# The head of a fused attention and feed-forward kernel: passes of one, two and two chunks, x loaded first, and a shorter warm-up

## The chip, the cores and the metric

The kernel runs on one core of a Trainium2 chip. The metric is the device time of one execution in microseconds (us). The engines are TensorE (PE, with its weight loads shown apart as PEld), VectorE (DVE), ScalarE (ACT), GpSimd (POOL) and SyncE (SP). SyncE computes nothing here: it issues the transfers between the chip's memory (DRAM) and SBUF, one after another, from one queue.

## The reference

x has 2048 tokens of 640 values, in bf16. Two branches work on the same x, and a gate mixes them by token:

```python
g = _sigmoid((x * gate_w).sum(-1, keepdims=True))
a = _A_ref(x, A_wqkv, A_w_phi, A_wo)      # linear attention, 32 heads of 20
b = _B_ref(x, B_w_gate, B_w_up, B_w_down) # (silu(x @ w_gate) * (x @ w_up)) @ w_down
return g * a + (1 - g) * b
```

Branch A projects x to q, k and v, multiplies q and k by a small matrix for each head, takes softmax of the result and of its negative as features, forms the feature-by-value matrix of each head over all tokens, and divides numerator by denominator for each token before the output projection `wo`. Branch B is a feed-forward layer with 1728 hidden values, which the kernel cuts into 14 tiles of up to 128.

## The kernel before, in words

The tokens are worked on in four blocks of 512. 640 values are 5 chunks of 128 rows, so a product with x for one hidden tile is 5 matmuls of 128x512 accumulated in one PSUM bank (of 8). x reaches SBUF transposed as `xT[128, chunk, token]`, by transposing transfers that SyncE issues (`load_x`, L509). The gate and up weights stand in `wg` and `wu` as `[128, chunk, column]`; `load_gu` (L504) loads them in pieces of columns, and the first 512 columns, four hidden tiles, are loaded by `load_head` (L532).

A small planner written in Python (`_Plan`, L237) fixes the order of the instructions on every engine when the program is built. Each task has an engine, a planned cost, dependencies, a priority, and PSUM banks or buffers that it takes and gives back. The planner simulates time: on each engine it takes the ready task of the best priority. A load has a planned landing time (`land`), and for landings over 13 us an extra slack (`L_SLACK`); `E_SLACK` and `O_SLACK` (L483) are extra time for the transposes inside the chip, of the features (`eT`) and of the attention output (`oT`). The Q and K tiles may not start before `K_AT + K_EACH * t` and `Q_AT + Q_EACH * t` (L707, L853). Only the order that comes out of this enters the program: on the chip, engines wait on semaphores for data that is truly there, not for planned times.

The stages, as the profile shows them: a warm-up of TensorE on a row of ones (L603 to L615), ten matmuls of 512 columns whose results nobody reads, from 0.8 us; the **head** (`ffn_head`, L677), the gate and up products of the first token block for the first four hidden tiles, 40 matmuls in 8 banks, until 13.8 us; further feed-forward tiles with the premultiplied projections; from about 30 us V and K tiles, with feed-forward tiles filling TensorE; from about 121 us Q tiles with numerator, output projection and down projections. Results are stored tile by tile to the end.

The order within the head is written out by hand. `group(key, c0, c1, parts)` makes a TensorE task for each tuple of hidden tiles in `parts`; a task runs the chunks c0 to c1 of its tiles, and waits for x of its last chunk and for its weights. The tasks are chained by `after`, so they run in the order written: gate chunks 0-1 for four tiles, up chunks 0-1 for four tiles, gate chunks 2-3 then 4 for tiles 0 and 1, gate chunks 2-4 for tiles 2 and 3, up chunks 2-4 tile by tile (L697 to L702). Behind them `ffn_tail` (L629) empties the banks: tanh of the gate and a copy of the up product on ACT, a combination on DVE, the product on POOL.

SyncE's queue starts with (L538 to L545): gate weights of chunks 0-1, x chunks 0-1, up weights of chunks 0-1, gate weights of chunks 2-4 for two tiles, x chunks 2-3, x chunk 4, gate weights of chunks 2-4 for the other two tiles, up weights of chunks 2-4, then the next piece of gate and up weights, and x of the second token block. The order follows the priorities, and `load` chains the loads of one engine.

All matmuls of the kernel other than the warm-up carry line L442 in the profile, all transfers L470, and most ACT operations L452.

Of the kernel before, what the change touches and what calls it, by code (L numbers as in the profile page):

```python
# [6 lines left out]
P = 128  # L7
# [29 lines left out]
class _Tracker:  # L37
# [123 lines left out]
    def run(self, eng, fn, reads=(), writes=(), semname=None, inc=None):  # L161
        rkeys = [self._key_of(a) for a in reads]
        wkeys = [self._key_of(a) for a in writes]
        need = {}

        def req(ev):
            if ev is None:
                return
            s, v = ev
            if v > need.get(s, 0):  # L170
                need[s] = v

        for k in rkeys:
            for kk in self._conflicts(k):
                req(self.lastw[kk])
        for k in wkeys:
            for kk in self._conflicts(k):
                req(self.lastw[kk])
                for s, v in self.readers[kk].items():
                    req((s, v))  # L180
        self._emit_waits(eng, need)
        ins = fn()
        if semname is None:
            semname = {"pe": "pe", "act": "act", "dve": "dve", "pool": "pool"}[eng]
            if inc is None:
                inc = 1
        elif semname == "dma":
            semname = self.new_dma_sem()
            inc = 16
        ins.then_inc(self.sem[semname], inc)  # L190
        self.cnt[semname] += inc
        v = self.cnt[semname]
        ev = (semname, v)
        snapd = dict(self.known[eng])
        if snapd.get(semname, 0) < v:
            snapd[semname] = v
        self.evknow.setdefault(semname, {})[v] = snapd
        for k in wkeys:
            self.lastw[k] = ev
            self.readers[k] = {}  # L200
        for k in rkeys:
            r = self.readers[k]
            if r.get(semname, 0) < v:
                r[semname] = v
        return ev
# [31 lines left out]
class _Plan:  # L237
# [11 lines left out]
    def add(self, eng, cost, fn, deps=(), prio=5.0, lat=None, acq=(), rel=(), name=""):  # L249
        t = _Task(eng, cost, fn, deps, prio, self.LAT[eng] if lat is None else lat,  # L250
                  tuple(acq), tuple(rel), len(self.tasks), name)
        self.tasks.append(t)
        return t
# [82 lines left out]
def _mm(*cols):  # L336
    return sum(c / 2400.0 + 0.003 for c in cols)


def _build(  # L340
# [13 lines left out]
    pe, act, dve, pool, sp = nc.tensor, nc.scalar, nc.vector, nc.gpsimd, nc.sync  # L354
    run = tr.run
# [54 lines left out]
    ps = nc.alloc_psum_tensor("ps", [P, 8 * 512], F32)  # L410
# [6 lines left out]
    add = plan.add  # L417
# [4 lines left out]
    def one(b, c0, c1, r0=0, r1=P):  # L422
        return ps[r0:r1, b * 512 + c0:b * 512 + c1]
# [4 lines left out]
    def mms(groups):  # L428

        reads = [g[1] for g in groups] + [g[2] for g in groups]  # L430
        writes = []
        seen = set()
        for g in groups:
            k = (g[0].offset, str(g[0].ap))
            if k not in seen:
                seen.add(k)
                writes.append(g[0])

        def fn():
            last = None  # L440
            for o, l, r, st, sp_ in groups:
                last = pe.matmul(o, lhsT=l, rhs=r, start=st, stop=sp_, skip_group_check=True)  # L442
            return last
        run("pe", fn, reads=reads, writes=writes)
# [21 lines left out]
    def dma(eng, dst, src, transpose=False, keep=False):  # L466
        eobj = tr.engobj[eng]
        reads = [src] if src.tensor.name in tr.addr else []
        writes = [dst] if dst.tensor.name in tr.addr else []
        fn = (lambda: eobj.dma_start(dst, src, transpose=True)) if transpose else (lambda: eobj.dma_start(dst, src))  # L470
        ev = run(eng, fn, reads=reads, writes=writes, semname="dma")
        if keep:
            out_evs.append(ev)
# [6 lines left out]
    v1ones = places(v1all)[:, :, :, DH]  # L480
    v1pad = v1all.rearrange("p (g x) -> p g x", x=WIN)[:, :, WIN - 1]

    L_SLACK, E_SLACK, O_SLACK = 1.0, 1.4, 1.0  # L483
    chain = {}

    def load(eng, dst, src, land, prio, transpose=False, name="load", cost=0.06):

        t = add(eng, cost, lambda: dma(eng, dst, src, transpose=transpose), prio=prio, lat=2.0, name=name)
        t.land = land
        t.slack = L_SLACK if land > 13 else 0.0  # L490
        t.after = chain.get(eng)
        chain[eng] = t
        return t
# [7 lines left out]
    wgl = [None] * (NPC + 1)  # L501
    wul = [None] * (NPC + 1)

    def load_gu(j, eng, land, prio):  # L504
        c0, c1 = PIECES[j]
        wgl[j] = load(eng, wg[:, :, c0:c1], gsrc[:, :, c0:c1], land[0], prio)
        wul[j] = load(eng, wu[:, :, c0:c1], usrc[:, :, c0:c1], land[1], prio + 0.1)

    def load_x(bt, prio, *cuts):  # L509

        tok = slice(512 * bt, 512 * bt + 512)
        out_ = []
        for i, (c0, c1, land) in enumerate(cuts):
            out_ += [load("sp", xT[:, c0:c1, tok], x2[tok, c0 * P:c1 * P], land, prio + 0.1 * i, True, "x%d" % bt)] * (c1 - c0)
        return out_
# [12 lines left out]
    xs = [None] * NBT  # L528
    HD = 4
    hw = {}  # L530

    def load_head(key, c0, c1, k0, k1, land, prio):  # L532
        w, src = (wg, gsrc) if key == "g" else (wu, usrc)
        t = load("sp", w[:, c0:c1, k0 * P:k1 * P], src[:, c0:c1, k0 * P:k1 * P], land, prio)
        for k in range(k0, k1):
            hw[key, c0, k] = t
        return t
    load_head("g", 0, 2, 0, HD, 3.9, -43)  # L538
    xa = load_x(0, -42, (0, 2, 5.25))
    load_head("u", 0, 2, 0, HD, 6.9, -41)  # L540
    load_head("g", 2, 5, 0, 2, 7.4, -40.5)
    xs[0] = xa + load_x(0, -40, (2, 4, 8.8), (4, 5, 9.3))
    wgl[0] = load_head("g", 2, 5, 2, HD, 10.0, -39.5)
    wul[0] = load_head("u", 2, 5, 0, HD, 11.3, -39)
    load_gu(1, "sp", (12.5, 13.7), -37)  # L545
    xs[1] = load_x(1, -36.5, (0, 5, 16.4))
    ph_l = load("sp", wph[:, :, :], rows(A_w_phi.rearrange("h e f -> (h e) f")), 16.5, -36.2)
    load_gu(2, "sp", (17.6, 18.8), -36)
# [51 lines left out]

    ones_row = nc.const_aps.tensor(1.0, (P, 512), BF16)

    def warm(banks, before):  # L603
        ctx = {}

        def fn():
            for b in banks:
                last = pe.matmul(one(b, 0, 512), lhsT=ones_row[:, 0:P], rhs=ones_row[:, 0:512], start=True, stop=True, skip_group_check=True)
            return last
        b0, b1 = min(banks), max(banks) + 1  # L610
        t = add("pe", 0.427 * len(banks), lambda: run("pe", fn, reads=[], writes=[ps[:, b0 * 512:b1 * 512]]), prio=-10,
                acq=[("bank", ctx, i) for i in range(b0, b1)], rel=[("bank", ctx, i) for i in range(b0, b1)], name="warm")
        t.after = before
        return t
    warm_t = warm((4, 5, 6, 7, 4, 5), warm((0, 1, 2, 3), None))  # L615


    gate_t = {}
# [58 lines left out]
    def ffn_head():  # L677
        tsl = slice(0, 512)
        cs = [{} for _ in range(HD)]
        before = warm_t  # L680
        last = {}

        def group(key, c0, c1, parts):
            nonlocal before
            w = wg if key == "g" else wu

            def fn(ks, cc):
                mms([(one(cs[k][key], 0, 512), w[:, c, P * k:P * k + P], xT[:, c, tsl], c == 0, c == 4) for c in cc for k in ks])
            for ks in parts:
                t = add("pe", _mm(*[512] * (len(ks) * (c1 - c0))), lambda ks=ks: fn(ks, range(c0, c1)),  # L690
                        deps=[xs[0][c1 - 1], hw[key, min(c0, 2), ks[-1]]], prio=-5,
                        acq=[("bank", cs[k], key) for k in ks] if c0 == 0 else (), name="head")
                t.after = before
                before = t
                for k in ks:
                    last[key, k] = t
        group("g", 0, 2, [(0, 1, 2, 3)])  # L697
        group("u", 0, 2, [(0, 1, 2, 3)])
        group("g", 2, 4, [(0, 1)])
        group("g", 4, 5, [(0, 1)])  # L700
        group("g", 2, 5, [(2, 3)])
        group("u", 2, 5, [(0,), (1,), (2,), (3,)])  # L702
        for k in range(HD):
            ffn_tail(0, k, cs[k], (last["g", k], last["u", k]), 0)

    B_FIRST = 8
    K_AT, K_EACH, Q_AT, Q_EACH = 30.0, 6.08, 120.8, 8.05  # L707
    PRE_Q = 10.06
    PRE_EACH = 2.2
    PRE_AT = 23.6  # L710
# [305 lines left out]
    pre_q = premult(0, wqT_l, PRE_Q, 0.02)  # L1016
    wq_done[0] = pre_q[-1]
    ffn_head()
    for bt in range(NBT):
        for t in range(4 * bt, 4 * bt + 4):  # L1020
# [6 lines left out]
    for bt in range(1, NBT):  # L1027
        ks = list(range(K_PAIRS if bt == 1 else 0, NK))
# [72 lines left out]
```

## Time and profile before

| | |
|---|---|
| median of 3 runs | 287.67 us (287.45 to 287.74) |
| span of the profiled execution, first to last instruction | 285.6 us |
| time of that execution outside the span | not listed; the median is 2.07 us over the span |
| TensorE busy | 282.2 us, 99% of the span |
| first matmul of the warm-up | 0.84 us |
| first matmul of the head | 5.17 us |
| first matmul after the head | 13.80 us |
| granted clock of TensorE, mean | 1.000 |

Times inside the profile are counted from the start of the span. A matmul's listed length holds its way through the array, and the next one starts before it ends; the pace is read from the starts. A transfer's instruction on SyncE (SPq) shows only its issue; its data move later, and the time "to landing" runs from the start of the issue to the last increment of its semaphore. "Idle before" names what ended an engine's idle time.

### The profile page before, as it was taken

How to read it: one execution, taken by the hardware profiler on the slowest of the kernel's cores; microseconds unless marked ns; L12 is line 12 of the kernel's file. 1: busy time of each engine (PE TensorE's matmuls, PEld its weight loads, DVE VectorE, ACT ScalarE, POOL GpSimd, SP SyncE). 2: the span in 40 equal slices, each digit the busy share in tenths (PEclk: the TensorE clock that was granted, in tenths of full speed). 3: DMA queues.
4: the chain of work that ended last, by engine and by line, in shares of the span. 5: the costliest groups of instructions: out<-in, count | busy, mean ns of one | idle time of the engine just before them, and what ended most of it. 6: DMA issues, size and time to landing. Idle time of an engine off the chain costs nothing.

```text
span 285.6 us, 5119 instructions
## 1 busy us (share of the span) xinstructions
PE 282.2 (99%) x2050; PEld 151.0 (53%) x2050; DVE 223.9 (78%) x318; ACT 146.2 (51%) x222; POOL 171.2 (60%) x164
## 2 busy tenths in 40 slices
PE   8999999999999999999999999999999999999996
PEld 3445555455555555655445555555455565545654
DVE  1324299999999999999999977989999978970312
ACT  2555656775756584344563454456655545564110
POOL 5199407686388748663684577676986666665100
DMA  7999999200000000000217517363435335323211
GB/s 178 258 234 268 225 187 330 88 1 1 2 0 2 0 0 2 2 0 0 45 20 82 127 50 143 75 95 76 93 79 96 67 66 117 60 39 75 69 48 46
DMA packets 65848, 23.91 MB, mean 84 GB/s; under 512 B 53984, under 2 KB 65824, under 8 KB 65824
## 3 DMA queue, kind: packets, MB, share of 16 engines
q1 hardware_dynamic: 65168, 23.58, 38.5%
q8 instruction: 16, 0.26, 0.4%
q10 hardware_dynamic: 656, 0.00, 0.1%
q14 instruction: 8, 0.07, 0.1%
HBM read 8.30 MB, written 2.62 MB: 38 GB/s over the span
## 4 chain that ended last, share of the span: by engine, by line
PE 97%; DMA 1%; SPq 0%; DVE 0%; issue 0%
PE ps L442 97%; DMA xT<-in_A_x_dram 1%; SPq L470 0%; DVE xsb L738 0%
## 5 line engine op out<-in xcount | busy, mean ns | idle before, releaser
L905 POOL TENSOR_TENSOR phi<-phi,rc 128x1320 bf16<-128x1320 bf16 x32 | 77.6, 2426 | 37.8 <-DVE rc L899 37.7
L654 POOL TENSOR_TENSOR hT<-hT,us 128x512 bf16<-128x512 bf16 (+1 forms) x56 | 64.1, 1154 | 41.8 <-DVE hT L648 21.2
L442 PE MATMUL ps<-xT,wg 128*128 128x512 bf16 x280 | 69.1, 379 | 0.2 <-DMA xT<-in_A_x_dram 0.2
L442 PE MATMUL ps<-xT,wu 128*128 128x512 bf16 x260 | 64.3, 379 | 0.0
L442 PE MATMUL ps<-wd,hT 128*128 128x512 bf16 (+1 forms) x448 | 63.0, 299 | 0.0
L648 DVE SCALAR_TENSOR_TENSOR hT<-hT,ps 128x512 bf16<-128x512 bf16 (+1 forms) x56 | 37.5, 674 | 20.4 <-ACT hT L452 20.4
L895 DVE TENSOR_REDUCE sm<-phi 128x66 f32<-128x1320 bf16 x32 | 48.5, 1517 | 6.2 <-ACT phi L452 6.0
L452 ACT ACTIVATE phi<-phi 128x1320 bf16<-128x1320 bf16 x32 | 41.6, 1301 | 17.9 <-DVE phi L884 17.6
L452 ACT ACTIVATE hT<-ps 128x512 bf16<-128x512 f32 (+1 forms) x56 | 33.1, 594 | 34.1 <-PE ps L442 33.6
L442 PEld LDWEIGHTS ps<-wd,hT 128*128 128x128 bf16 x448 | 35.0, 98 | 26.9
L442 PE MATMUL ps<-wqk,xT 128*128 128x512 bf16 (+1 forms) x320 | 48.5, 299 | 0.0
L452 ACT ACTIVATE us<-ps 128x512 bf16<-128x512 f32 (+1 forms) x56 | 33.2, 597 | 17.2 <-PE ps L442 15.7
L442 PEld LDWEIGHTS ps<-xT,wu 128*128 128x128 bf16 x260 | 25.3, 98 | 30.9 <-issue 0.3
L442 PEld LDWEIGHTS ps<-xT,wg 128*128 128x128 bf16 x280 | 25.7, 98 | 25.9 <-issue 0.8
L442 PEld LDWEIGHTS ps<-wqk,xT 128*128 128x128 bf16 x320 | 26.2, 98 | 21.2 <-ACT hT L452 0.2
L872 DVE TENSOR_REDUCE mx<-ps 128x33 f32<-128x660 f32 x32 | 26.8, 837 | 9.3 <-PE ps L442 9.2
L452 ACT ACTIVATE xsb<-ps,gs 128x640 bf16<-128x640 f32 x16 | 12.7, 795 | 32.3 <-PE ps L442 32.3
L884 DVE TENSOR_TENSOR phi<-mn,ps 128x660 bf16<-128x660 f32 x32 | 26.3, 821 | 0.4
L880 DVE TENSOR_TENSOR phi<-ps,mx 128x660 bf16<-128x660 f32 x32 | 26.3, 821 | 0.0
L876 DVE TENSOR_REDUCE mn<-ps 128x33 f32<-128x660 f32 x32 | 26.2, 819 | 0.0
L752 POOL TENSOR_TENSOR xsb<-xsb,xb 128x640 bf16<-128x640 bf16 x12 | 16.7, 1395 | 14.3 <-ACT xb L452 14.3
L442 PE MATMUL ps<-wo,oT 128*128 128x512 bf16 (+1 forms) x160 | 24.3, 299 | 0.0
(44 smaller groups left out, 187.9 us busy)
## 6 DMA issues: line engine op xcount, KB each, us to landing
out_dram<-xsb SPq DMA_DIRECT2D x15, 160.0 KB, 2.0
wd<-in_B_w_down_dram SPq DMA_DIRECT2D x1, 2080.0 KB, 9.4
wg<-in_B_w_gate_dram SPq DMA_DIRECT2D x2, 400.0 KB, 4.1
wu<-in_B_w_up_dram SPq DMA_DIRECT2D x2, 400.0 KB, 4.9
wvg<-in_A_wqkv_dram SPq DMA_DIRECT2D x1, 800.0 KB, 6.9
wo<-in_A_wo_dram SPq DMA_DIRECT2D x1, 800.0 KB, 10.7
wg<-in_B_w_gate_dram SPq DMA_DIRECT2D x2, 320.0 KB, 4.2
wu<-in_B_w_up_dram SPq DMA_DIRECT2D x2, 320.0 KB, 4.8
```

The costliest lines, as they stand in the source:

```text
L442: last = pe.matmul(o, lhsT=l, rhs=r, start=st, stop=sp_, skip_group_check=True)
L452: run("act", lambda: act.activation(o, i, func, scale=scale), reads=reads, writes=[o])
L648: dveop(lambda: dve.scalar_tensor_tensor(out=hap, in0=hap, scalar=1.0, in1=g_, op0=ALU.add, op1=ALU.mult), [hap, g_], [hap])
L654: poolop(lambda: pool.tensor_tensor(hap, hap, u_, ALU.mult), [hap, u_], [hap])
L752: poolop(lambda: pool.tensor_tensor(x_, x_, b_, ALU.add), [x_, b_], [x_])
L872: dveop(lambda: dve.tensor_reduce(a, b, AX.X, ALU.max), [b], [a])
L876: dveop(lambda: dve.tensor_reduce(a, b, AX.X, ALU.min), [b], [a])
L880: dveop(lambda: dve.tensor_tensor(o_, a, b, ALU.subtract), [a, mx[:, ctx["st"], :]], [o_])
L884: dveop(lambda: dve.tensor_tensor(o_, a, b, ALU.subtract), [b, mn[:, ctx["st"], :]], [o_])
L895: dveop(lambda: dve.tensor_reduce(a, b, AX.X, ALU.add), [b], [a])
L905: poolop(lambda: pool.tensor_tensor(a, a, b, ALU.mult), [a, r], [a])
```

## The change

The five chunks of the head are worked on in three passes: chunk 0, chunks 1-2, chunks 3-4, each with the gate product before the up product, for all four hidden tiles. The loads are cut at the same places, 9 in place of 8: x, gate weights, up weights of each pass in turn, x first. All are still issued by SyncE. The warm-up has 8 matmuls of 384 columns in place of 10 of 512. The planned landing times, the planned cost of the first gate pass, `E_SLACK`, `O_SLACK`, and the holds of the K and Q tiles get new values, and the planner makes a new order from them.

```diff
-    L_SLACK, E_SLACK, O_SLACK = 1.0, 1.4, 1.0
+    L_SLACK, E_SLACK, O_SLACK = 1.0, 1.6, 1.4
...
-    def load_head(key, c0, c1, k0, k1, land, prio):
+    HEAD_C = (0, 1, 3, 5)
+
+    def load_head(eng, key, i, land, prio):
         w, src = (wg, gsrc) if key == "g" else (wu, usrc)
-        t = load("sp", w[:, c0:c1, k0 * P:k1 * P], src[:, c0:c1, k0 * P:k1 * P], land, prio)
-        for k in range(k0, k1):
-            hw[key, c0, k] = t
-        return t
-    load_head("g", 0, 2, 0, HD, 3.9, -43)
-    xa = load_x(0, -42, (0, 2, 5.25))
-    load_head("u", 0, 2, 0, HD, 6.9, -41)
-    load_head("g", 2, 5, 0, 2, 7.4, -40.5)
-    xs[0] = xa + load_x(0, -40, (2, 4, 8.8), (4, 5, 9.3))
-    wgl[0] = load_head("g", 2, 5, 2, HD, 10.0, -39.5)
-    wul[0] = load_head("u", 2, 5, 0, HD, 11.3, -39)
-    load_gu(1, "sp", (12.5, 13.7), -37)
+        c0, c1 = HEAD_C[i], HEAD_C[i + 1]
+        hw[key, i] = load(eng, w[:, c0:c1, 0:HD * P], src[:, c0:c1, 0:HD * P], land, prio, cost=0.5 if eng == "act" else 0.06)
+        return hw[key, i]
+    xs[0] = load_x(0, -43, (0, 1, 3.6))
+    load_head("sp", "g", 0, 4.0, -42.5)
+    load_head("sp", "u", 0, 4.6, -42.4)
+    xs[0] = xs[0] + load_x(0, -42, (1, 3, 5.9))
+    load_head("sp", "g", 1, 6.4, -41)
+    load_head("sp", "u", 1, 7.0, -40.5)
+    xs[0] = xs[0] + load_x(0, -40, (3, 5, 8.2))
+    wgl[0] = load_head("sp", "g", 2, 8.9, -39.5)
+    wul[0] = load_head("sp", "u", 2, 9.5, -39)
+    load_gu(1, "sp", (11.5, 12.7), -37)
...
+    WARM_N = 384
...
-                last = pe.matmul(one(b, 0, 512), lhsT=ones_row[:, 0:P], rhs=ones_row[:, 0:512], start=True, stop=True, skip_group_check=True)
+                last = pe.matmul(one(b, 0, WARM_N), lhsT=ones_row[:, 0:P], rhs=ones_row[:, 0:WARM_N], start=True, stop=True, skip_group_check=True)
...
-        t = add("pe", 0.427 * len(banks), lambda: run("pe", fn, reads=[], writes=[ps[:, b0 * 512:b1 * 512]]), prio=-10,
+        t = add("pe", 0.32 * len(banks), lambda: run("pe", fn, reads=[], writes=[ps[:, b0 * 512:b1 * 512]]), prio=-10,
...
-    warm_t = warm((4, 5, 6, 7, 4, 5), warm((0, 1, 2, 3), None))
+    warm_t = warm((4, 5, 6, 7), warm((0, 1, 2, 3), None))
...
+            i = HEAD_C.index(c0)
             for ks in parts:
-                t = add("pe", _mm(*[512] * (len(ks) * (c1 - c0))), lambda ks=ks: fn(ks, range(c0, c1)),
-                        deps=[xs[0][c1 - 1], hw[key, min(c0, 2), ks[-1]]], prio=-5,
+                t = add("pe", _mm(*[512] * (len(ks) * (c1 - c0))) * (1.0 if c0 or key == "u" else 1.6), lambda ks=ks: fn(ks, range(c0, c1)),
+                        deps=[xs[0][c1 - 1], hw[key, i]], prio=-5,
...
-        group("g", 0, 2, [(0, 1, 2, 3)])
-        group("u", 0, 2, [(0, 1, 2, 3)])
-        group("g", 2, 4, [(0, 1)])
-        group("g", 4, 5, [(0, 1)])
-        group("g", 2, 5, [(2, 3)])
-        group("u", 2, 5, [(0,), (1,), (2,), (3,)])
+        for i in range(2):
+            for key in "gu":
+                group(key, HEAD_C[i], HEAD_C[i + 1], [(0, 1, 2, 3)])
+        group("g", 3, 5, [(0, 1), (2, 3)])
+        group("u", 3, 5, [(0,), (1,), (2,), (3,)])
...
-    K_AT, K_EACH, Q_AT, Q_EACH = 30.0, 6.08, 120.8, 8.05
+    K_AT, K_EACH, Q_AT, Q_EACH = 30.00, 6.147, 121.50, 8.058
```

## The prediction, made before the changed kernel ran

> **What bounds the kernel now.** I read the page's first line of busy times, then the chain that ended last, then the PE waits, and only then the timeline of the head.
>
> ```profile
> span 285.6 us, 5119 instructions
> PE 282.2 (99%) x2050; PEld 151.0 (53%) x2050; DVE 223.9 (78%) x318; ACT 146.2 (51%) x222; POOL 171.2 (60%) x164
> ```
>
> ```profile
> 1.32 3.72 DMA xT<-in_A_x_dram
> 5.04 0.14 issue
> 5.17 278.13 PE ps L442 x2040
> 283.31 0.02 issue
> 283.33 0.35 DVE xsb L738
> ```
>
> The chain says it all: one transfer of x lands at 5.04, and from 5.17 to 283.31 TensorE runs 2040 matmuls with nothing between them. The list of PE waits has only two entries, 0.8 us before the warm-up and 0.2 us for that x. So the time is (moment at which useful matmuls start) + 278.1 us of matmuls + a tail of 2.3 us + any idle time or half-speed time that PE gets after its start. The diff changes no useful matmul, so only the start, and idle or slow time after it, can move the end. The whole time of the profiled execution is not listed beside its span; the median of the three runs, 287.67, is 2.07 us over the span. I take these 2.07 us as unchanged and add differences to 287.67. A measurement of this kernel can tell about 0.2% (0.57 us) from no change.
>
> The stage that the diff rewrites, in the timeline (start, length, engine, what):
>
> ```profile
> 0.80 0.45 SPq L470 DMA_DIRECT2D wg<-in_B_w_gate_dram  x1
> 0.84 4.09 PE L608 MATMUL ps<-const-bfloat16-1.0 128*128 128x512 bf16 x10 [0.84 <-PEq L1085]
> 1.32 1.32 SPq L470 DMA_TRANSPOSE xT<-in_A_x_dram  x1
> 2.69 0.57 SPq L470 DMA_DIRECT2D wu<-in_B_w_up_dram  x1
> 3.31 0.46 SPq L470 DMA_DIRECT2D wg<-in_B_w_gate_dram  x1
> 3.82 2.53 SPq L470 DMA_TRANSPOSE xT<-in_A_x_dram  x2
> 5.17 1.89 PE L442 MATMUL ps<-xT,wg 128*128 128x512 bf16 x8 [0.24 <-DMA xT<-in_A_x_dram]
> 6.90 1.89 PE L442 MATMUL ps<-xT,wu 128*128 128x512 bf16 x8
> 8.65 4.80 SPq L470 DMA_TRANSPOSE xT<-in_A_x_dram  x1
> 13.80 1.24 PE L442 MATMUL ps<-xT,wg 128*128 128x512 bf16 x5
> ```
>
> Two rates come from here. Eight head matmuls start every 1.73 us (5.17 to 6.90), 0.216 us each, and the head's 40 take 8.63 us, until 13.80. And SyncE, which issues every load, needs 1.2 to 1.3 us for a transpose whether it holds one chunk of x or two (1.32 for two; 2.53 for one of two and one of one), and 0.45 to 0.58 us for a plain load.
>
> **The part that starts earlier.** The change's first load is x chunk 0. Laid out with these issue times (1.26 for a transpose, 0.57 for a plain load after one, 0.48 for the next, 0.05 between): x0 issued at 0.80, g0 at 2.11, u0 at 2.73, x1-2 at 3.25, g1-2 at 4.53, u1-2 at 5.15, x3-4 at 5.68, g3-4 at 6.97, u3-4 at 7.60. How long from issue to landing?
>
> ```profile
> out_dram<-xsb SPq DMA_DIRECT2D x15, 160.0 KB, 2.0
> wg<-in_B_w_gate_dram SPq DMA_DIRECT2D x1, 256.0 KB, 2.9
> wu<-in_B_w_up_dram SPq DMA_DIRECT2D x1, 256.0 KB, 3.4
> out_dram<-xsb SPq DMA_DIRECT2D x1, 128.0 KB, 1.7
> ```
>
> The 256 KB rows are today's first gate load (nothing ahead of it) and first up load (behind a transpose). No load of 128 KB exists; the nearest rows are the output stores, 1.7 us for 128 KB and 2.0 for 160 KB. For g0 and u0 (128 KB) I take 1.95, with ends 1.7 and 2.9. So g0 lands at 4.06 (3.8 to 5.0), x0 long before it (a transpose of five blocks, oT, lands after 2.6 us, so about 3.4), and the first useful matmul starts at 4.2, given the 0.13 us between landing and matmul seen above (5.04 to 5.17). u0 lands at 2.73 + 1.95 = 4.7, before the gate pass ends. PE therefore starts 0.97 us earlier. If nothing else happened, that would be the gain.
>
> **The part that is late next.** The first two passes hold only 4 + 4 matmuls now, 1.73 us at full speed, where before they held 8 + 8 (3.46 us). PE is through them at 5.9 to 6.4. The next pass needs x1-2 and g1-2. x1-2 is issued at 3.25 and would land 2.9 us later at 6.15 (an unhindered transpose of eleven blocks, eT, takes 3.5 to 3.6 in its rows, of five blocks 2.6; eight blocks lie between). g1-2 is 256 KB issued at 4.53. Its bounds are 2.0 us (the 160 KB store) and 3.4 us (the up load behind a transpose, which is its exact position). I take 2.4: the store's 2.0 plus 96 KB more at the 234 to 311 GB/s that the DMA windows of the head show, 0.3 to 0.4 us. I choose it nearer to the store because the queues ahead of it are emptier than they were for today's up load: only 640 KB are issued before it, and SyncE's issue time leaves holes. So g1-2 lands at 6.93 (6.5 to 7.9) and its matmuls start at 7.06 (6.7 to 8.1). 32 matmuls are left, 6.91 us: the head ends at **13.97** (13.6 to 15.0) against 13.80, which is **+0.17 us** (-0.2 to +1.2). Later passes do not bind: u1-2, issued at 5.15, is needed at 8.8; g3-4 (6.97) at 10.5, u3-4 (7.60) at 12.2, each 3.5 us or more after issue. So the 0.97 us gained at the start come back as a hole of about 0.7 to 1.1 us before the second gate pass.
>
> **What the shorter warm-up costs.** Today the ten warm-up matmuls start 0.427 us apart (two of them span 1.06 us from 3.36) until the ninth; the tenth follows 0.34 us after it, and useful matmuls run at 0.216 from the first. So PE went to full speed at about 4.46, 3.6 us after its first matmul, though the column of the granted clock reads 1.00 all along:
>
> ```profile
> 0.80:4.20 3.40, 3.36 (x8) 1.00 0.70 151
> 4.20:4.60 0.40, 0.40 (x3) 1.00 0.99 162
> ```
>
> With eight matmuls of 384 columns (0.427 x 384/512 = 0.32 each) the warm-up ends at 0.84 + 2.56 = 3.4, and PE rests 0.8 us until 4.2. If full speed still comes at 4.46, the useful matmuls lose (4.46 - 4.2)/2 = 0.13 us; if it comes later, half of each further microsecond. But the hole before 7.06 hides it: the two small passes end at 5.93 plus half the slow time, so slowness until 6.46 costs nothing. I put this term at 0, under the cover of the late g1-2 load; without the cover it is 0.13 to 0.5 us. The diff's own planning cost (the first gate pass times 1.6, 0.52 us more) would fall in this hidden part too.
>
> The Trainium skill, "TensorE: Matmul & The Clock Gate", Part 1 on the HAM clock gate, speaks against the shorter warm-up: the gate opens after a busy window of about 3.4 us whose phase is free, and the page advises 4 us or more of matmuls without a break. The 3.6 us of this trace agree with that; what a warm-up of 2.6 us and a pause does is shown by no row here. By that rule the time is that of rival B below.
>
> **Behind the head.** SyncE has one more plain load ahead of chunk loads for later work, so everything after moves up to 0.6 us later (x of the second token block issued at 9.26 for 8.65). Its consumers have cover: that x landed at 16.45 (8.65 + 7.8) and PE asks for it two pairs of 2.16 us after the head, 18.3; the next weight pair landed at 12.05 and 13.3 (7.55 + 4.5, 8.08 + 5.2) and is asked for at 13.97 and 15.05; wkT landed at 22.05, asked for at 24.4. Taken at 0. The tails of the four head groups are compressed: the last up group now follows its gate group by less. Four tanh and four copies of 0.60 us on ACT and four DVE steps of 0.69 us start 2.6 us before the head's end; the first bank comes free about 1.3 us before PE wants one, and then one every 0.6 us for a demand of one every 1.08 us. Also 0.
>
> The rewritten planning constants (holds for the K and Q tiles, slacks for the transposes) reorder the following 270 us. PE has no idle time there to win, so this can only lose. For a loss speaks that DVE leaves hardly any room in the middle:
>
> ```profile
> 60.00:120.00 60.00, 60.00 (x485) 33.00 (x484) 59.39 (x79) 35.76 (x58) 42.29 (x36) 1.00 0.00 1
> 120.00:200.00 80.00, 80.00 (x622) 43.63 (x620) 73.65 (x107) 39.80 (x51) 50.66 (x41) 1.00 0.36 64
> ```
>
> (PE, PEld, DVE, ACT, POOL busy.) Against it: the K interval grows from 6.08 to 6.147, so less DVE work is asked for per microsecond, and more slack for the transposes means waits less often. Taken at 0.
>
> **Sum:** 287.67 - 0.97 (first useful matmul at 4.2 instead of 5.17) + 1.13 (hole before the second gate pass, with any slow clock inside it: 7.06 less 5.93, where the first passes would end) = **287.83**, so 287.8.
>
> **Rivals.**
> A. The loads are quick enough that PE never waits after its start. Then the head ends at 4.2 + 8.63 plus 0.13 of slow clock, 12.96: -0.84, **286.8**. It needs g1-2 at 6.0, 1.5 us after its issue; 1.7 us for half the bytes speaks against it. The landing of 6.4 that the diff writes down for g1-2 would give 13.44 or 287.3, still under 0.2%. To gain 0.57 us it must land by 6.2. Faster also if SyncE issues one-chunk transposes in less time than 1.2 us.
> B. The other side: the pause cancels the warm-up. If the 3.6 us count anew from 4.2, full speed comes at 7.8, the eight small matmuls run at 0.427 until 7.6, and the second gate pass starts there, still slow for 0.2 us: the head ends at 7.6 + 6.91 + 0.1 = 14.6, +0.8, **288.5**. It decides from 6.46 on, as worked out above. If the hole before 7.06 restarts the count once more, half of 3.6 us is added instead: 15.8, +2.0, 289.7. For it: no such pause is in the trace of before. Against it: by 4.46 PE would have been busy for 2.8 of 3.6 us.
> C. The new order of the later stages stalls PE. Sixteen K tiles at 0.067 us more each put the last one 1.0 us later; if PE ran dry for that, +1.0, with the head's 0.17 **288.8**.
>
> **Chances.** Forecast 0.54, within 0.2%; A 0.13, faster; B 0.20 and C 0.13, slower. So faster 0.13, same 0.54, slower 0.33. The range 287.0 to 289.0 reaches into A, holds B's first price and C, and leaves out A's full gain and B's double price. The forecast's own range is 287.4 to 288.3 (g1-2 landing from 6.5 to 7.4).
>
> **What would show it.** In the timeline after: first useful matmul at 4.2; a PE wait of about 1 us ahead of the second gate pass, released by DMA wg; the first matmul that is no head matmul at 14.0; matmul starts 0.216 apart by 6.5. Wrong if PE waits under 0.3 us in all (A), if matmuls 0.427 apart go on past 6.5 (B), if PE waits behind 30 us (C), or if a one-chunk transpose is issued in well under 1.2 us.

## The result, and the profile after

The changed kernel takes 289.28 us (median of 6 runs, 288.56 to 289.67) against 287.71 us for the kernel before (6 runs, 287.45 to 288.02). The ratio is 1.0051, with a 95% interval of 1.0041 to 1.0061: it is slower, by about 1.5 us. The forecast was 287.8 with a range up to 289.0.

The page's first lines, and the list of PE waits:

```profile
span 287.6 us, 5077 instructions
PE 280.9 (98%) x2011; PEld 151.0 (53%) x2048; DVE 224.3 (78%) x318; ACT 145.2 (50%) x222; POOL 171.2 (60%) x164
```

```profile
PE ps L442 <- DMA wg<-in_B_w_gate_dram: 1.5, 2, 1.1
PE ps L613 <- PEq L1090: 0.8, 1, 0.8
```

There are fewer matmuls in the list than before because the warm-up has two fewer and 37 of this trace's matmul records are missing (2048 weight loads stand beside 2011 matmuls); a missing one shows as a start-to-start distance of 0.43 us in place of 0.216. The waits are what counts: 1.5 us in two waits, both for gate weights (total, times, longest), where before there was one of 0.2 us for x.

The head in the timeline of PE:

```profile
0.84 2.72 PE L613 MATMUL ps<-const-bfloat16-1.0 128*128 128x384 bf16 x8 [0.84 <-PEq L1090]
4.62 1.89 PE L442 MATMUL ps<-xT,wg 128*128 128x512 bf16 x4 [1.06 <-DMA wg<-in_B_w_gate_dram]
6.30 1.90 PE L442 MATMUL ps<-xT,wu 128*128 128x512 bf16 x4
8.67 1.90 PE L442 MATMUL ps<-xT,wg 128*128 128x512 bf16 x8 [0.47 <-DMA wg<-in_B_w_gate_dram]
10.41 1.89 PE L442 MATMUL ps<-xT,wu 128*128 128x512 bf16 x8
...
15.59 1.24 PE L442 MATMUL ps<-xT,wg 128*128 128x512 bf16 x4
```

Read the starts. Useful work begins at 4.62 instead of 5.17. But the first four matmuls need 1.68 us (4.62 to 6.30), 0.42 us each, half speed, and so do the next four. Then comes a wait, and the second gate pass starts at 8.67. From there on it is 0.216 us each, and the head ends at 15.59, against 13.80: +1.79 us. Behind the head little was lost: from the head's end to the start of the last matmul it is 269.43 us here and 269.27 us before, +0.16 us. The chain that ended last goes through the same place:

```profile
4.46 0.58 SPq L470 DMA_DIRECT2D wg<-in_B_w_gate_dram  x1
```

```profile
3.17 1.25 SPq L470
4.46 4.16 DMA wg<-in_B_w_gate_dram
8.67 7.30 PE ps L442 x33
```

(The first fence is from the timeline, the second from the chain.) The gate weights of chunks 1-2 were issued at 4.46, where the prediction had 4.53, and landed 4.16 us later, at 8.63, where it had 2.4 us later. So either their landing costs the time, or the slow clock, which by itself kept the first eight matmuls busy until 8.0.

### The profile page after: what moved, and what is told of

Read it like the earlier page. It is cut to its first block, busy times and chain, and to the rows that moved or that the text cites. A ratio compares the mean times of both kernels' runs of the same rounds, so it can differ in the third digit from the quotient of the medians.

```text
span 287.6 us, 5077 instructions
## 1 busy us (share of the span) xinstructions
PE 280.9 (98%) x2011; PEld 151.0 (53%) x2048; DVE 224.3 (78%) x318; ACT 145.2 (50%) x222; POOL 171.2 (60%) x164
## 4 chain that ended last, share of the span: by engine, by line
PE 96%; DMA 1%; SPq 1%; issue 1%; DVE 0%
PE ps L442 96%; DMA wg<-in_B_w_gate_dram 1%; SPq L470 1%; DVE xsb L743 0%
## 5 line engine op out<-in xcount | busy, mean ns | idle before, releaser
L442 PE MATMUL ps<-wd,hT 128*128 128x512 bf16 (+1 forms) x442 | 62.3, 298 | 0.3
L442 PE MATMUL ps<-wqk,xT 128*128 128x128 bf16 (+1 forms) x312 | 47.6, 297 | 0.4
L442 PE MATMUL ps<-wo,oT 128*128 128x128 bf16 (+1 forms) x153 | 23.0, 295 | 0.4
```

## The experiments

Ratios are against the kernel before, timed on the same chip; 0.1% is 0.29 us. All kernels start from the changed kernel ("after") or the one before, as said.

### First set: which part of the change costs?

**Long warm-up in the changed kernel** (e1). Only the warm-up is set back:

```diff
-    WARM_N = 384
+    WARM_N = 512
-    warm_t = warm((4, 5, 6, 7), warm((0, 1, 2, 3), None))
+    warm_t = warm((4, 5, 6, 7, 4, 5), warm((0, 1, 2, 3), None))
```

> The changed kernel with the warm-up of before (ten matmuls of 512 columns, no pause); every instruction order else is the changed kernel's. Theory L (the second gate pass waits for its weights, which land at 8.63 us whatever TensorE does): the two small passes end at about 6.6 us at full speed, the wait before the second gate pass grows from 0.5 to about 2 us, the head ends at 15.6 as in the changed kernel, and the time stays at 289.3 us, within 0.2. Theory C (the slow clock of the two small passes is the loss): the head ends about 1.1 to 1.7 us earlier, 287.6 to 288.2 us.

Measured 289.30 us, ratio 1.0051 (1.0039 to 1.0063), the same as the changed kernel. In its trace full speed came only at about 6.8, although the warm-up ran without a break until the first useful matmul, and the wait grew:

```profile
5.06 1.87 PE L442 MATMUL ps<-xT,wg 128*128 128x512 bf16 x4
6.77 1.03 PE L442 MATMUL ps<-xT,wu 128*128 128x512 bf16 x4
8.85 1.90 PE L442 MATMUL ps<-xT,wg 128*128 128x512 bf16 x8 [1.05 <-DMA wg<-in_B_w_gate_dram]
```

The small passes are through earlier, at about 7.6, but the weights of the second gate pass landed at 8.80. Theory L holds: the landing bounds, and the slow clock is hidden in front of it.

**The old planning constants in the changed kernel** (e2).

```diff
-    L_SLACK, E_SLACK, O_SLACK = 1.0, 1.6, 1.4
+    L_SLACK, E_SLACK, O_SLACK = 1.0, 1.4, 1.0
-    K_AT, K_EACH, Q_AT, Q_EACH = 30.00, 6.147, 121.50, 8.058
+    K_AT, K_EACH, Q_AT, Q_EACH = 30.0, 6.08, 120.8, 8.05
```

> The changed kernel with the planning constants of before (slacks of the transposes, holds of the K and Q tiles), so another order behind about 30 us. Theory: the new order costs and gains nothing, since TensorE has no idle time behind the head in either trace: 289.3 us, within 0.2. Rival: part of the 1.6 us lies in the new order; then this one is at least 0.4 us faster than the changed kernel.

Measured 290.06 us, ratio 1.0073 (1.0061 to 1.0085): neither theory; it is slower than the changed kernel, by intervals that just touch. Its profile shows 269.77 us from the head's end to the last matmul, 0.34 us more than the changed kernel, with weight loads that wait 0.6 us for ACT's writes of `xsb`. The head of that execution ended 0.68 us later too, at 16.27, where these constants change no order: its weights landed at 8.86, and full speed came as late as 9.9, which cost 0.46 us after the wait. So part of the 0.2% may be the head of single executions; how it divides is not settled.

**The short warm-up in the kernel before** (e3); its diff is the warm-up part of the change alone.

> The kernel before with the short warm-up alone (eight matmuls of 384 columns, end at 3.4 us, a pause of 1.8 us until x lands at 5.04). Theory C: the pause starts the count anew, full speed comes 3.4 to 3.6 us after 5.17, the head's first eight matmuls start 0.427 us apart, the head ends 1.7 us later, 289.4 us. Theory of a clock that comes at about 4.5 to 5 us whatever the pause: 287.7 us, within 0.3.

Measured 288.98 us, ratio 1.0034 (1.0019 to 1.0050), and the ten runs lie between 287.51 and 289.78. The profiled one, at 289.78, shows theory C, and more of it:

```profile
0.84 2.72 PE L608 MATMUL ps<-const-bfloat16-1.0 128*128 128x384 bf16 x8 [0.84 <-PEq L1085]
5.38 3.57 PE L442 MATMUL ps<-xT,wg 128*128 128x512 bf16 x8 [1.82 <-DMA xT<-in_A_x_dram]
8.75 2.38 PE L442 MATMUL ps<-xT,wu 128*128 128x512 bf16 x8
```

Eight matmuls take 3.37 us (5.38 to 8.75), and full speed comes near 9.7; the head ends at 16.15, 2.35 us later than before, where the theory had 1.7. The fastest run is as fast as the kernel before, so in some executions it seems to come in time. The short warm-up does cost about 1 us on average, where no late load covers it.

**The gate weights of chunks 1-2 ahead of their x** (e4), in the changed kernel:

```diff
+    load_head("sp", "g", 1, 6.4, -42.2)
     xs[0] = xs[0] + load_x(0, -42, (1, 3, 5.9))
-    load_head("sp", "g", 1, 6.4, -41)
```

> The changed kernel with one load moved: the gate weights of chunks 1-2 are issued ahead of x of chunks 1-2, right behind the small up load. Theory L (SyncE's issue of a transpose, 1.25 us, and the slow start of a plain stream behind a transpose delay these weights): the weights land at about 6.2, x of chunks 1-2 at about 7.5, and the second gate pass starts when the slow small passes end, at 8.0 instead of 8.67: 0.6 us faster than the changed kernel, 288.7 us. Rival (the transfers are bound by bytes alone, so the order among them does not matter): second gate pass still at about 8.7, 289.3 us.

Measured 289.09 us, ratio 1.0038 (1.0025 to 1.0051). The weights landed at 6.36 and x at 7.40, as theory L had it, and the second gate pass ran without a wait; but it started at 8.27, right behind small passes that ran at half speed throughout, and its first matmul was slow too:

```profile
8.27 2.11 PE L442 MATMUL ps<-xT,wg 128*128 128x512 bf16 x8
```

With the landing cured, the clock is the next bound in this trace. Of the expected 0.6 us only 0.2 (medians) to 0.4 (ratios) came out, and the interval overlaps that of the changed kernel, so the times alone do not show a gain. In the trace the pair that the second gate pass needs, weights and x, was there at 7.40 instead of 8.63. That speaks against the rival, bytes alone, by which the order would not matter.

### Second set: is it the time in which SyncE issues?

**Two issuing queues** (e5): the six gate and up loads of the changed head go to ScalarE's queue, `load_head("act", ...)`. **The same with the long warm-up** (e6).

> The changed kernel with the six gate and up loads of the head issued by ScalarE's queue, so that SyncE issues only transposes there; nothing else differs. Theory I (what makes the second gate pass late is the time in which one queue issues: x of chunks 1-2 and these weights are issued at 3.2 and 4.5 us, and the transfers run dry before): issued at about 1.8, the weights land by 6.5 us, the second gate pass follows the first passes without a wait for a transfer, and the head ends at 14.9 or earlier, by when the clock comes: at most 288.6 us. Rival (the transfers are bound by bytes or by slow starts of a stream, whoever issues them): second gate pass at 8.6 again, 289.3 us.

> The run before with the long warm-up of the kernel before in addition. If the slow clock of the first passes is what holds the head once the loads are early, this one is faster than the one with two queues alone by 0.3 to 0.8 us, about 288.0 us. If loads still hold it, there is no difference, within 0.2.

Measured 291.40 us (ratio 1.0113, 1.0086 to 1.0140) and 290.78 us (1.0108, 1.0085 to 1.0131). Theory I falls, and so does its rival: it got worse. By the ratios the long warm-up makes no difference, and the trace of e6 says why: full speed came at 4.3, and the second gate pass still waited 2.4 us for x. The list of PE waits of e5, then two stretches of e5 (length, granted clock, share of the transfer engines, GB/s):

```profile
PE ps L442 <- DMA xT<-in_A_x_dram: 3.0, 3, 1.4
```

```profile
1.75:4.25 2.50, 1.00 0.98 239
4.25:8.50 4.25, 1.00 1.16 171
```

The issue of all nine loads has begun by 3.5 us, but x lands late: x of chunks 1-2 at 9.33, 7.2 us after its issue, where one queue took 3.6. The transfer engines move 171 GB/s although they are busy throughout. So issuing early from two queues did not make the loads land early. Why the transposes and the plain loads of two queues come this slowly is not shown.

**x first in the kernel before** (e7): its first two loads exchanged.

> The kernel before with its first two loads exchanged: x of chunks 0-1 first, then gate weights of chunks 0-1; all else as before, with the long warm-up. Theory: x lands at about 4.2 instead of 5.04, but the weights, issued at 2.1, land at about 5.3, so the head starts 0.1 to 0.4 us later: 287.8 to 288.3 us. Rival (x first is what costs, since the transfers start later): over 288.6 us.

Measured 288.28 us, ratio 1.0020 (1.0011 to 1.0028). In its trace x landed at 4.12, but the gate weights, issued at 2.20 behind it, only at 6.00, so the head began at 6.05:

```profile
6.05 1.90 PE L442 MATMUL ps<-xT,wg 128*128 128x512 bf16 x8 [1.42 <-DMA wg<-in_B_w_gate_dram]
```

The same 256 KB that landed 2.9 us after their issue as the very first load (3.3 in e3) take 3.8 us behind a transpose. x first costs 0.2% even without the division in three.

**The kernel before with two queues and eight warm-up matmuls** (e8).

> The kernel before with the five gate and up loads of the head issued by ScalarE's queue and a warm-up of eight matmuls of 512 columns, which ends at about 4.25 us: x of chunks 0-1, issued first by SyncE, lands at about 4.2, the head starts at 4.3 and nothing waits after that. While the clock is low the useful matmuls run at half speed, so 0.3 to 0.6 us of the 0.87 us are left: 287.2 to 287.6 us, faster than both kernels. If the pieces that share the transfer engines slow each other (x landing after 5.0), it is 287.9 us or later.

Measured 290.44 us, ratio 1.0103 (1.0081 to 1.0125): the second branch. x of chunks 0-1, issued at 0.80, landed at 6.73. That is only part of the loss in the profiled execution:

```profile
6.87 3.57 PE L442 MATMUL ps<-xT,wg 128*128 128x512 bf16 x8 [2.45 <-DMA xT<-in_A_x_dram]
10.23 2.83 PE L442 MATMUL ps<-xT,wu 128*128 128x512 bf16 x8
```

Its head starts 1.7 us later than before and ends 4.3 us later (18.07 against 13.80); the other 2.6 us are matmuls at half speed until about 12.1, behind a warm-up that ended 2.45 us before the first useful matmul. This run does not price the two queues alone.

### Third set: the parts one by one

**Weights of chunks 1-2 first, and the long warm-up** (e9: e1 and e4 together).

> The run with the gate weights of chunks 1-2 ahead of their x, with the long warm-up in addition. Theory of two bounds in a row (a plain stream that starts right behind a transpose is slow, so the weights come late; behind that bound lies the clock): with the weights early, the second gate pass now waits only for x of chunks 1-2, at about 7.5 us, and the first passes are through by then whenever the clock comes; head end about 14.6, time 288.4 to 288.6 us, 0.5 us faster than without the long warm-up. If the clock is no bound there, 289.1 us as before.

Measured 288.71 us, ratio 1.0032 (1.0021 to 1.0042): 0.06% under e4, where 0.17% was expected, and no difference by the intervals. In its trace full speed came at about 6.8, the weights landed at 7.17 and x at 8.20, each 0.8 us later than in e4 with the same loads in the same order; the second gate pass waited 0.5 us for x and began at 8.34. The transfers of the two traces differ from 6.0 to 7.0 us, where these loads move, e9 first, e4 second (length, clock, share, GB/s):

```profile
6.00:7.00 1.00, 1.00 1.04 55
```

```profile
6.00:7.00 1.00, 1.00 1.14 217
```

The engines are busy in both, and move 55 GB/s in one and 217 in the other. Why is open; the landing in one trace is uncertain by as much as these 0.8 us.

**The first gate load of the kernel before cut by chunk** (e10): gate chunk 0, x of chunks 0-1, gate chunk 1, the rest as before, with nine warm-up matmuls.

> The kernel before with its first gate load cut by chunk (chunk 0 first, then x of chunks 0-1, then gate weights of chunk 1, the rest as before) and nine warm-up matmuls for ten. By the bytes, x lands 0.3 to 0.5 us earlier and the head starts at 4.7; then the weights of chunk 1, 128 KB right behind a transpose, must land by 5.6. If they do: head end 13.4, 287.4 us, the fastest. If the slow start behind a transpose holds them until 6.0 or later: no gain or a loss, 287.9 to 288.2 us.

Measured 288.02 us, ratio 1.0009 (1.0001 to 1.0018): no gain. x landed at 4.83, only 0.2 us earlier; the weights of chunk 1, behind it, at 6.33, 3.7 us after their issue for 128 KB. Time and landing are those of the second branch, but in the profiled execution nothing waited for these weights:

```profile
4.96 2.76 PE L442 MATMUL ps<-xT,wg 128*128 128x512 bf16 x8
```

The four matmuls of chunk 0 ran at half speed until 6.62, past the landing, and full speed came at about 6.8. So here the clock set the pace, and the run does not price the late landing.

**Division in three, weights ahead of x, long warm-up** (e11). Of the change's head this keeps the division:

```diff
-    xs[0] = load_x(0, -43, (0, 1, 3.6))
-    load_head("sp", "g", 0, 4.0, -42.5)
+    load_head("sp", "g", 0, 4.0, -43.5)
+    xs[0] = load_x(0, -43, (0, 1, 3.6))
...
```

and so in the other two passes.

> The changed kernel with the gate weights ahead of x in each of the three passes, and with the long warm-up: of the change, the division in three alone. Theory: gate weights land before their x, the first useful matmul runs at about 5.1 when the warm-up ends, the second gate pass at about 7.5; 288.3 to 288.6 us, so dividing in three alone still costs 0.5 to 0.8 us. If x first is the whole loss, 287.8 us.

Measured 288.14 us, ratio 1.0013 (1.0004 to 1.0021), between the two branches. Between e1 and this kernel only the place of the gate weights differs, and that is 0.38% (1.0051 to 1.0013), **1.1 us**. What is left against the kernel before is one wait, now for x:

```profile
5.00 1.03 PE L442 MATMUL ps<-xT,wg 128*128 128x512 bf16 x4
5.87 1.03 PE L442 MATMUL ps<-xT,wu 128*128 128x512 bf16 x4
7.50 1.89 PE L442 MATMUL ps<-xT,wg 128*128 128x512 bf16 x8 [0.61 <-DMA xT<-in_A_x_dram]
```

**The new planning constants in the kernel before** (e12; the reverse of the diff of e2).

> The kernel before with the new planning constants alone (slacks, holds of the K and Q tiles). Theory: another order with no idle time of TensorE, 287.8 us within 0.2. Rival: the new constants are themselves worth or cost over 0.3 us.

Measured 287.81 us, ratio 1.0005 (0.9996 to 1.0015): no difference. In its trace it is 269.44 us from the head's end to the start of the last matmul, 0.17 more than before and the same as in the changed kernel (269.43).

### Fourth set: is it the transpose?

**Plain loads in place of x's transposes, with a small load behind each** (e13), and **the same without the small loads** (e14), both with the long warm-up:

```diff
+    def plain_x(i, prio, land):
+        c0, c1 = HEAD_C[i], HEAD_C[i + 1]
+        t = load("sp", xT[:, c0:c1, 0:512], usrc[:, c0:c1, 512:1024], land, prio)
+        load("sp", padt[:, i, :], gsrc[:, i, 0:2], land, prio + 0.01)   # in e13 alone
+        return [t] * (c1 - c0)
```

> The changed kernel with the long warm-up, and with the three transposes of x in the head replaced by plain loads of the same size (up weights in place of x, so the first token block is not computed from x), each followed by a plain load of 4 bytes per partition so that SyncE's issue takes about 1.0 us for the pair, near the transpose's 1.25. Theory T (a plain load behind a transpose is slow because of the transpose): the gate weights of chunks 1-2 land 2.4 to 3.2 us after their issue instead of 4.2, by 7.2 us, and the time is 288.0 us or less. Rival (they are late because the first loads are small and issued with gaps, whatever their kind): 3.8 us or more after issue, 288.8 us or more.

> The run with plain loads in place of the transposes, without the small loads that filled SyncE's issue time, so that the head's nine loads are one unbroken row of plain loads (the first token block is again not computed from x). If a plain stream is slow whenever it begins, after a transpose, a small load or a gap alike, then here only the first load is slow, the gate weights of chunks 1-2 land 2.4 to 3.2 us after their issue (by 6.0 us), TensorE waits under 0.3 us in the head, and the time is 287.9 us or less. If these weights are slow to come whatever stands ahead of them, they need 3.8 us or more again, and the time is 288.2 us or more.

e13: 288.51 us, ratio 1.0024 (1.0013 to 1.0035). Theory T falls: with no transpose in the head, the gate weights of chunks 1-2, issued at 3.65 behind a load of 4 bytes per partition, landed 4.35 us later, at 8.00. The time lies between the two branches; issue took 0.9 to 1.0 us for the pair, less than a transpose's 1.25, so these weights were issued 0.8 us earlier than in the changed kernel.

e14: 287.15 us, ratio 0.9986 (0.9976 to 0.9997). PE does not wait in the head:

```profile
5.06 1.07 PE L442 MATMUL ps<-xT,wg 128*128 128x512 bf16 x4
5.97 1.03 PE L442 MATMUL ps<-xT,wu 128*128 128x512 bf16 x4
6.83 1.89 PE L442 MATMUL ps<-xT,wg 128*128 128x512 bf16 x8
```

The time and the waits are those of the first theory; its landing is not: the weights land 3.9 us after issue, at 6.60, behind 640 KB that were issued in a row. The two differ in the stretch where these weights move, e13 first, e14 second (length, clock, share, GB/s):

```profile
5.00:6.25 1.25, 1.00 0.80 128
6.25:8.00 1.75, 1.00 1.02 320
```

```profile
5.00:6.25 1.25, 1.00 1.02 330
6.25:8.00 1.75, 1.00 1.08 366
```

In e13 these 1.25 us, in which the small load ends and the weights' stream begins, move 128 GB/s; in e14 they lie in the middle of an unbroken row and move 330. But an unbroken row is not free of such a stretch. This is e14 a little earlier:

```profile
3.50:4.50 1.00, 1.00 0.79 172
```

The changed kernel has the same pattern, with a transpose for the small load:

```profile
4.50:6.00 1.50, 1.00 0.80 168
6.00:7.25 1.25, 1.00 0.80 147
7.25:8.50 1.25, 1.00 1.27 312
```

x of chunks 1-2 until about 6.0, then the slow beginning of the weights until 7.25, then 312 GB/s. That the break itself makes the stretch slow is argued from these windows, not shown: of the 1.40 us by which e14's weights land earlier than e13's, 0.99 are their earlier issue (2.66 for 3.65), and the runs do not separate the rest from the break. What e13 does show is that no transpose is needed for the late landing. e14 is no version to use, since it does not load x; of the kernels that compute everything none was faster than the kernel before.

## Why the prediction was wrong

- **What bounds the kernel**: right for this change. Its head's end moved the time by 1.79 us and all that follows by 0.16, and the chain runs through transfers of the head and then PE. The 2.07 us between span and time were too much by 0.4: the profiled run after took 289.30 us with a span of 287.6, and in every experiment the two differ by 1.7 to 1.8. They were the median of three runs less the span of one execution, which must have been quicker than the median.
- **Useful work starts 0.97 us earlier, at 4.2**: it was 4.62, 0.55 us earlier. x landed at 3.42 as worked out; g0 took 2.47 us instead of 1.95. The store row, 1.7 us for 128 KB, was no measure for a load behind a transpose; the other end, 2.9, held. x of chunks 1-2 landed at 6.77, not 6.15, and bound nothing.
- **The step that failed: "g1-2 lands at 6.93 (6.5 to 7.9) and its matmuls start at 7.06 (6.7 to 8.1)"**. It landed at 8.63, 4.16 us after issue; 2.4 was taken, and even the upper bound, 3.4 from "its exact position", was short. That row's load stands third in the queue, behind one transpose; g1-2 stands fifth, behind two. Two loads of the kernel's head that also stand behind transposes were in the same list of the kernel before and were not used:

```profile
wg<-in_B_w_gate_dram SPq DMA_DIRECT2D x2, 192.0 KB, 3.3
wu<-in_B_w_up_dram SPq DMA_DIRECT2D x1, 384.0 KB, 3.8
```

256 KB lie between them. With 3.5 us, an estimate from these two rows, the second gate pass starts at about 8.2 and the sum gives 288.9 us: most of the miss.

The reason given for the low choice, "the queues ahead of it are emptier", pointed the wrong way. What the runs showed in its place: behind x of the same chunks these 256 KB landed 4.2 to 4.4 us after their issue (the changed kernel, e1, e2), and ahead of x after 3.2 to 4.0 us (e4, e9, e11). Emptier queues meant engines that stood idle, not a quicker load: between 1.9 and 6.3 us the kernel before moved 239 GB/s, e11 183, the changed kernel 154.

The three rows are one window each, in that order (length, clock, share, GB/s):

```profile
1.90:6.30 4.40, 1.00 1.02 239
```

```profile
1.90:6.30 4.40, 1.00 0.78 183
```

```profile
1.90:6.30 4.40, 1.00 0.68 154
```

The rate falls with the engines' share (1.02, 0.78, 0.68), and divided by it all three move 226 to 235 GB/s. So these windows show idle engines and no slower packets. Why the weights of the changed kernel then came at 147 GB/s from 6.00 to 7.25 stays open.

- **The kind of loss** was right: the start gained comes back in front of the second gate pass, released by the gate weights. The sum by its terms: -0.55 for the start and 8.67 - (4.62 + 1.73) = +2.32 for hole and slow clock together make +1.77, against -0.97 and +1.13. The forecast was slower by 0.16 us; it came out slower by 1.5.
- **The short warm-up at 0 under cover**: right in the sum, by e1, but by luck. The term stood on half speed that ends by 6.46; it lasted until after the first eight matmuls, which were through at 8.0, rival B's case. Had the weights landed at 6.93 as forecast, the second gate pass would still have started at 8.0 or later (8.27 in e4, with weights and x there at 7.40), some 0.9 us after the 7.06 of the sum. Only the late landing hid this second miss. Without cover it costs 1.0 us on average (e3; the text gave 0.13 to 0.5). The Trainium skill, "TensorE: Matmul & The Clock Gate", Part 1 on the HAM clock gate, says that a window of some 3.4 us with free phase decides; its section "Why this matters for your kernels" advises to keep TensorE busy for 4 us or more. The traces agree on the free phase: full speed came at 4.5 (before), 6.8 (e1), 8.7 (e4), 9.7 (e3) and 9.9 us (e2) from one and the same first matmul at 0.84, and e3's runs spread over 2.3 us, while the kernel before, whose warm-up has no such pause, spreads over 0.7 us in the 15 runs beside them. They do not bear out 4 us as always enough: in e1 and e9 matmuls followed each other from 0.84 without a break, and full speed came 5.9 us later.
- **Behind the head, 0 for transfers, tails and constants**: right within 0.2 us for the changed kernel (269.43 against 269.27 us); e12 finds no effect of the constants alone on the time. That the old constants come out slower with the new head (e2) was not foreseen.
- **Rivals**: A needed the weights at 6.0 and was far off. B's half speed took place but was hidden. C did not happen. Missing among them was the one that came: that the weights behind x and its transpose land later than any row that was taken as a bound.

The parts in numbers: x ahead of the weights 1.1 us (e1 against e11), the division in three with the constants 0.13%, some 0.4 us (e11), the constants nothing measurable (e12), the short warm-up nothing here (e1) and 1.0 us where it is not covered (e3).

## What to carry to other kernels

In a start that is fed by one queue, try the weights ahead of x: here that alone was worth 1.1 us (e1 against e11). Cutting loads small to start earlier can land the next ones later, and an early first matmul gains nothing if the second group's load sets the time. When a hole is forecast behind an earlier start, size it from the slowest row that stands at the same place in the queue, and not from a row of an idle queue. And do not put a cost at nothing because another, itself forecast, will cover it: in these runs the warm-up that ends in a pause was free only while a later wait covered it, and became the bound where the weights came early (e4).

## What the runs showed that was not expected

Early in the kernel a stream of plain loads has slow stretches: 128 and 147 GB/s for 1.25 us behind a break (e13, after), with or without a transpose in front, and 172 GB/s for 1 us in an unbroken row (e14), against 312 to 366 GB/s once it runs. With transposes and plain loads from two queues the transfer engines moved 171 GB/s while fully busy (e5). The Trainium skill, "DMA: Bandwidth & Descriptors", "Issuing engines are not separate DMA queues", says that issuing from several engines only saves issue time; here the saving came with a loss of 2 us (291.40 against 289.28), for a reason that the runs do not show.

SyncE needs 1.21 to 1.34 us to issue a transpose of one chunk or of two in the head, in all kernels with one queue (once 1.61, in e9). And the column of the granted clock reads 1.00 through the half-speed stretches; the pace of the starts shows them.
